# A transformer block on one core: the first chunk's normalization in an order written by hand, three MLP blocks ahead of the projections

## The chip, the cores and the metric

The kernel runs on one core of a Trainium2 chip. The core has a matrix engine (TensorE, PE in the profile; its weight loads are PEld), a vector engine (VectorE, DVE), a scalar engine (ScalarE, ACT), a general engine (GpSimd, POOL) and a queue engine (SyncE, SP) that issues most transfers. Each engine takes its instructions in the order in which they are written for it, and waits on semaphores for the others. SBUF is the on-chip memory, PSUM the accumulation memory that PE writes. The metric is the device time of one execution in microseconds (us).

## What is computed

x has 2048 rows of 1024 elements in bf16. It is normalized by rows, and the result goes into two branches: an attention of 32 heads in which each position sees eight earlier ones, two apart, and a gated MLP of width 3584.

```python
xn = _layernorm(x, axis=-1)                  # (x - mean) / sqrt(var + 1e-5)
s = _A_ref(xn, A_wqkv, A_wo)                 # qkv, 8 positions at distance 2, softmax, @ wo
g = _silu(_B_ref(xn, B_w1, B_w3, B_w2))      # silu((silu(xn@w1) * (xn@w3)) @ w2)
return x + s * g
```

## The kernel before

The rows are cut into four chunks of 512 (`CH`), each of four tiles of 128 rows. For a chunk the work is: `ln_transpose` (statistics and normalization of the four tiles, then eight 128x128 transposes on PE for each, copied by ACT into `xnT`, lines 122 to 140), `qkv` (24 accumulations `ps` of eight matmuls each, line 159, copied by ACT into qT, kT and vT, line 170), `attention` (on DVE: products `prod` and sums into `E`, lines 177 to 180; an exchange of partitions by GpSimd's transfers, line 184; the softmax, lines 188 to 201; transfers back, line 204; products with v summed into `oT`, lines 211 to 226), `wo_proj` (eight accumulations of eight matmuls, line 241, copied by ACT into `s_sb`, line 247), `mlp_up` (14 blocks; a block loads one tile of w1 and one of w3, fills four accumulations `gu` on line 264, and ACT's silu `sg` and DVE's product `ht` free them, lines 271 and 273), and `mlp_down_epilogue` (for both halves `dh` of the columns, four accumulations `acc_0_*` and `acc_1_*` of 28 matmuls each, line 324, and an `epilogue` for each).

An epilogue loads a piece `x_e` of x (line 281, GpSimd's queue), takes the silu of the accumulation on ACT into `gt` (line 289), multiplies by `s_sb` and adds `x_e` on DVE (lines 290 and 291), and stores `o_t` (line 292, GpSimd's queue). `x_e`, `gt` and `o_t` have two buffers each (the pool "ep").

The loop over chunks (lines 352 to 363) writes `ln_transpose` of the next chunk ahead of `mlp_down_epilogue`. The order on each engine isn't that of the text: a scheduler takes the instructions of the whole program and sets an order for each engine by its own estimate of when they are ready; `high_priority` moves some ahead. The order is then fixed. The accumulations of `mlp_up`, `qkv` and `mlp_down` share six banks of PSUM ("mm"), those of `wo_proj` and of the transposes two ("aux").

Chunk 0 differs. Its tiles are normalized one by one (`group=1`), and its first MLP block (`M1A = 1`) works in two halves of 256 columns (`nsplit=2`), so that it needs only two of the four tiles at first. Its projection weights come as six tiles `raw` (line 102; three buffers), which DVE and ACT permute in 24 copies of 128x1024 into three tiles `pm` (line 107); `qkv` of chunk 0 reads them from there, and three stores write them to DRAM as `wperm` (line 340) for the later chunks. Three further MLP blocks (`M1B = 4`) follow `qkv` before attention. Ahead of everything PE runs twelve matmuls on zeros (line 71).

Of the kernel before, what the change touches and what calls it, by code (L numbers as in the profile page):

```python
# [1 line left out]

# [5 lines left out]
FP32 = mybir.dt.float32  # L8
BF16 = mybir.dt.bfloat16
ACTF = mybir.ActivationFunctionType  # L10
ALU = mybir.AluOpType
# [4 lines left out]
def kernel(  # L16
# [11 lines left out]
    nc = tc.nc  # L28
    P = 128
    S, D, F = 2048, 1024, 3584  # L30
    Dh, W, DIL = 32, 8, 2
    KT = D // P
    CH = 512
    NCH = S // CH
    NST = CH // P
# [1 line left out]
    HALO = 16  # L37
    NWARM = 12
    M1B = 4
    M1A = 1  # L40
    NJ = 8
    NR = 4
    scale = float(Dh) ** -0.5

    x_flat = A_x.rearrange("b s d -> (b s) d")
    out_flat = out.rearrange("b s d -> (b s) d")
    w1_r = B_w1.rearrange("(kt p) f -> p kt f", p=P)
    w3_r = B_w3.rearrange("(kt p) f -> p kt f", p=P)
# [5 lines left out]
    psum_mm = ctx.enter_context(tc.tile_pool(name="psum_mm", bufs=6, space=bass.MemoryType.PSUM))  # L54
    psum_aux = ctx.enter_context(tc.tile_pool(name="psum_aux", bufs=2, space=bass.MemoryType.PSUM))
    ln = ctx.enter_context(tc.tile_pool(name="ln", bufs=2))
    small = ctx.enter_context(tc.tile_pool(name="small", bufs=4))
    xnT_pool = ctx.enter_context(tc.tile_pool(name="xnT", bufs=2))
    wstream = ctx.enter_context(tc.tile_pool(name="wstream", bufs=6))
# [3 lines left out]
    eps_t = const.tile([P, 1], FP32, name="eps_t")  # L63
    nc.vector.memset(eps_t[:], 1e-5)
    warm = const.tile([P, CH], BF16, name="warm")
    nc.vector.memset(warm[:], 0.0)
    scr = const.tile([P, 1], FP32, name="scr")
    nc.scalar.activation(out=scr[:], in_=eps_t[:], func=ACTF.Sqrt)
    wps = psum_aux.tile([P, CH], FP32, tag="aux", name="warm_ps")
    for _ in range(NWARM):  # L70
        nc.tensor.matmul(wps[:], lhsT=warm[:, 0:P], rhs=warm[:], start=True, stop=True)
    ident = const.tile([P, P], BF16, name="ident")
    nc.gpsimd.memset(ident[:], 0.0)
    nc.gpsimd.affine_select(
        out=ident[:], in_=ident[:], compare_op=ALU.not_equal, fill=1.0,
# [5 lines left out]
        out=maskb[0:32], in_=maskb[0:32], compare_op=ALU.is_ge, fill=-1.0e9,  # L81
# [9 lines left out]
    hp = ctx.enter_context(tc.tile_pool(name="hT", bufs=FT + 1))  # L91
    sgp = ctx.enter_context(tc.tile_pool(name="sg", bufs=3))
# [2 lines left out]

    wqkv_r = A_wqkv.rearrange("(kt kp) c -> kp kt c", kp=P)

    def permute_load(stage, t):
        pm = stage.tile([P, KT, NJ, P], BF16, tag="pm", bufs=3)
        for half in range(2):  # L100
            raw = stage.tile([P, 4, D], BF16, tag="raw", bufs=3)
            nc.sync.dma_start(out=raw[:], in_=wqkv_r[:, half * 4:(half + 1) * 4, t * D:(t + 1) * D])
            for k4 in range(4):
                kt = half * 4 + k4
                src = raw[:, k4, :].rearrange("k (h r j) -> k j r h", r=NR, j=NJ)
                dst = pm[:, kt, :, :].rearrange("k j (r h) -> k j r h", r=NR)
                PERM_ENG[(t * KT + kt) % len(PERM_ENG)](out=dst, in_=src)
        return pm

    PERM_ENG = [nc.vector.tensor_copy, nc.scalar.copy, nc.vector.tensor_copy]  # L110

    def ln_transpose(c, group=NST):
        xnT = xnT_pool.tile([P, KT, CH], BF16, tag="xnT")
        mv = small.tile([P, NST, nc.vector.BN_AGGR_DIM], FP32, tag="mv")
        rstd = small.tile([P, NST], FP32, tag="rstd")
        for st0 in range(0, NST, group):
            sts = range(st0, st0 + group)
            x_ts = {}
            for st in sts:
                g = c * NST + st  # L120
                x_t = ln.tile([P, D], BF16, tag="x_t", bufs=NST)
                nc.sync.dma_start(out=x_t[:], in_=x_flat[g * P:(g + 1) * P, :])
                stats = small.tile([P, 2, nc.vector.BN_STATS_DIM], FP32, tag="stats")
                for i in range(2):
                    nc.vector.bn_stats(out=stats[:, i, :], in_=x_t[:, i * 512:(i + 1) * 512])  # L125
                nc.vector.bn_aggr(out=mv[:, st, :], in_=stats[:])
                x_ts[st] = x_t
            sl = slice(st0, st0 + group)
            nc.scalar.activation(out=rstd[:, sl], in_=mv[:, sl, 1], func=ACTF.Sqrt, bias=eps_t[:], scale=1.0)
            nc.vector.reciprocal(out=rstd[:, sl], in_=rstd[:, sl])  # L130
            for st in sts:
                xn = ln.tile([P, D], BF16, tag="xn")
                nc.vector.tensor_scalar(
                    out=xn[:], in0=x_ts[st][:], scalar1=mv[:, st, 0:1], scalar2=rstd[:, st:st + 1],
                    op0=ALU.subtract, op1=ALU.mult,
                )
                tp = psum_aux.tile([P, KT, P], BF16, tag="aux")
                for kt in range(KT):
                    nc.tensor.transpose(tp[:, kt, :], xn[:, kt * P:(kt + 1) * P], ident[:])  # L139
                nc.scalar.copy(out=xnT[:, :, st * P:(st + 1) * P], in_=tp[:])  # L140
        return xnT

    def qkv(c, xnT, pms=None):
        if c > 0:
# [102 lines left out]
                    nc.scalar.copy(out=s_sb[:, st, dh * 512:(dh + 1) * 512], in_=ps[:])  # L247
        return s_sb

    def mlp_up(c, xnT, fb0, fb1, nsplit=1):  # L250
        hts = []
        cw = CH // nsplit
        for fb in range(fb0, fb1):
            w1t = wstream.tile([P, KT, 2 * P], BF16, tag="w")
            nc.sync.dma_start(out=w1t[:], in_=w1_r[:, :, fb * 256:(fb + 1) * 256])
            w3t = wstream.tile([P, KT, 2 * P], BF16, tag="w")
            nc.sync.dma_start(out=w3t[:], in_=w3_r[:, :, fb * 256:(fb + 1) * 256])
            pss = [psum_mm.tile([P, CH], FP32, tag="mm", name=f"gu{c}_{fb}_{k}") for k in range(4)]
            order = [(sp, k) for sp in range(nsplit) for k in range(4)] if nsplit > 1 else [(0, k) for k in range(4)]
            for sp, k in order:  # L260
                i, wt = k // 2, (w1t if k % 2 == 0 else w3t)
                cs = slice(sp * cw, (sp + 1) * cw)
                for kt in range(KT):
                    nc.tensor.matmul(  # L264
                        pss[k][:, cs], lhsT=wt[:, kt, i * P:(i + 1) * P], rhs=xnT[:, kt, cs],
                        start=(kt == 0), stop=(kt == KT - 1),
                    )
            for i in range(2):
                with tc.high_priority():
                    sg = sgp.tile([P, CH], BF16, tag="sg")  # L270
                    nc.scalar.activation(out=sg[:], in_=pss[2 * i][:], func=ACTF.Silu)
                    ht = hp.tile([P, CH], BF16, tag="ht")
                    nc.vector.tensor_mul(ht[:], sg[:], pss[2 * i + 1][:])  # L273
                hts.append(ht)
        return hts

    def epilogue(c, st, dh, acc, s_sb, nh=1):
# [51 lines left out]
                epilogue(c, st, dh, accs[st], s_sb)  # L329

    pools = {}
    xnT_cur = ln_transpose(0, group=1)
    hts0 = []
    with tc.tile_pool(name="stage", bufs=1) as stage:
        hts0 += mlp_up(0, xnT_cur, 0, M1A, nsplit=2)
        pms = [permute_load(stage, t) for t in range(3)]
        qkv(0, xnT_cur, pms)
        hts0 += mlp_up(0, xnT_cur, M1A, M1B)
        for t in range(3):
            nc.sync.dma_start(  # L340
                out=wperm[:, :, t * NJ:(t + 1) * NJ, :].rearrange("kt kp j p -> kp kt (j p)"),
                in_=pms[t][:].rearrange("kp kt j p -> kp kt (j p)"),
            )
# [8 lines left out]
    for c in range(NCH):  # L352
        if c > 0:
            qkv(c, xnT_cur)
        oT = attention(c)
        s_sb = wo_proj(c, oT)
        if c == 0:
            hts = hts0 + mlp_up(c, xnT_cur, M1B, FT // 2)
        else:
            hts = mlp_up(c, xnT_cur, 0, FT // 2)  # L360
        xnT_next = ln_transpose(c + 1) if c + 1 < NCH else None
        mlp_down_epilogue(c, hts, s_sb)
        xnT_cur = xnT_next

# [29 lines left out]
```

## Time and profile before

| | us |
|---|---|
| median of 3 runs (lowest, highest) | 841.57 (841.38, 841.77) |
| span of the profiled execution, first to last instruction | 841.2 |
| PE busy | 819.3 |
| DVE busy | 477.1 |
| ACT busy | 213.9 |
| POOL busy | 123.7 |
| mean granted clock of PE, as a share of full | 0.990 |

The profile shows one execution. Its span is 0.2 us below the lowest of the runs and 0.4 below their median; its own time with what lies around the span isn't given. A line of the timeline gives the start, the duration, the engine, the line of the kernel, the operation, what it writes and reads, the shape, the count, and in brackets how long the engine stood idle before it and what released it. A line of waits gives who waited for whom, the total, how often, and the longest. In a table of stretches each line has the stretch, its length, the busy time and number of instructions of PE, PEld, DVE, ACT and POOL, the granted clock, the share of the 16 DMA engines and GB/s.

Where the stages lie in the profiled execution:

| stage of chunk 0 | us from the start of the span |
|---|---|
| first matmul of MLP block 0 | 12.69 |
| qkv of chunk 0 on PE | 20.97 to 62.57 |
| MLP blocks 1 to 13 on PE | 62.41 to 159.47 |
| acc_0 and the first 52 matmuls of acc_1 | 159.47 to 194.90 |
| wo_proj | 194.90 to 208.71 |
| transposes of chunk 1 and the other 60 of acc_1 | 208.71 to 223.86 |
| qkv of chunk 1 begins | 223.86 |

### The profile page before, as it was taken

The page shows a single profiled execution, that of the slowest core. Times are in us where ns is not written, and L with a number is a line of the kernel's source. Part 1 is how long each engine was busy: PE and PEld are TensorE (multiplying, and loading weights), DVE is VectorE, ACT ScalarE, POOL GpSimd, SP SyncE. Part 2 cuts the span into 40 slices and gives each one's busy share as a digit, 9 for nine tenths or more (in the row PEclk, how much of TensorE's full clock was granted, in tenths as well). Part 3 has the DMA queues.
Part 4 walks back from the last instruction along what each step waited for, and adds up shares of the span by engine and source line. Part 5 has one row for each costly group of instructions (what it writes and reads, how often), then busy time and mean ns, then how long its engine had stood idle before and what let it go on. Part 6 is the DMA issues. An engine that isn't in the chain of part 4 may idle for free.

```text
span 841.2 us, 9707 instructions
## 1 busy us (share of the span) xinstructions
PE 819.3 (97%) x3884; PEld 377.0 (45%) x3884; DVE 477.1 (57%) x488; ACT 213.9 (25%) x325; POOL 123.7 (15%) x210
## 2 busy tenths in 40 slices
PE   7999889999999999999999999999999999999995
PEld 5444334444444444444444444444444444444442
DVE  7429946595239835494143955379302693629811
ACT  6742113103343113102233212210403311310120
POOL 1002133003100224002120040401102004120011
PEclk8999999999999999999999999999999999999998
DMA  9999397746595596754675577855476559593320
GB/s 302 314 358 230 102 226 173 190 150 176 130 289 149 153 201 183 177 164 119 193 239 150 148 170 185 202 154 167 114 213 200 151 150 200 159 205 112 109 81 25
DMA packets 208525, 149.54 MB, mean 178 GB/s; under 512 B 7776, under 2 KB 196192, under 8 KB 208480
## 3 DMA queue, kind: packets, MB, share of 16 engines
q1 hardware_dynamic: 201296, 132.14, 57.2%
q0 software_dynamic: 7184, 16.79, 8.0%
q8 instruction: 30, 0.49, 0.3%
q14 instruction: 15, 0.12, 0.1%
HBM read 130.02 MB, written 10.49 MB: 167 GB/s over the span
## 4 chain that ended last, share of the span: by engine, by line
PE 80%; DVE 15%; issue 3%; DMA 1%; ACT 0%; POOL 0%; POOLq 0%; DVEq 0%
PE ps L159 20%; PE ps L241 7%; DVE oT L226 2%; DVE B L225 2%; DVE C L211 2%; DVE B L211 2%; DVE ht L273 1%; DVE prod L177 1%; DMA x_t<-in_A_x_dram 1%; PE tp L139 1%; DVE oT L219 1%; PE acc_1_3_1668 L324 1%; PE acc_1_2_6323 L311 1%; PE acc_1_0_4763 L324 1%; PE acc_0_2_1505 L324 1%
## 5 line engine op out<-in xcount | busy, mean ns | idle before, releaser
L264 PEld LDWEIGHTS <-w3t 128*128 128x128 bf16 x912 | 89.8, 98 | 111.4 <-issue 7.8
L264 PEld LDWEIGHTS <-w1t 128*128 128x128 bf16 x912 | 89.6, 98 | 104.6 <-issue 0.2
L159 PE MATMUL ps<-xnT,wt 128*128 128x512 bf16 x576 | 124.8, 379 | 0.0
L324 PEld LDWEIGHTS <-ht 128*128 128x128 bf16 x784 | 76.4, 98 | 90.0 <-issue 0.2
L177 DVE TENSOR_TENSOR prod<-qT,kT 128x4096 bf16<-128x4096 bf16 x32 | 72.6, 2286 | 41.8 <-ACT kT L170 40.9
L159 PEld LDWEIGHTS <-wt 128*128 128x128 bf16 x576 | 56.3, 98 | 68.0
L290 DVE TENSOR_TENSOR gt<-gt,s_sb 128x512 f32<-128x512 f32 (+1 forms) x33 | 21.6, 673 | 77.0 <-ACT gt L289 64.3
L125 DVE BATCH_NORM_STATS2 stats<-x_t 128x6 f32<-128x512 bf16 x32 | 20.5, 671 | 58.4 <-DMA x_t<-in_A_x_dram 58.4
L204 POOL DMA_DIRECT2D E_persist<-pb x64 | 36.9, 584 | 100.1 <-DVE pb L201 93.3
L292 POOL DMA_DIRECT2D out_dram<-o_t x33 | 18.2, 551 | 205.9 <-DVE o_t L291 204.4
L159 PE MATMUL ps<-xnT,pm 128*128 128x512 bf16 x192 | 41.6, 379 | 0.0
L241 PEld LDWEIGHTS <-oT 128*128 128x128 bf16 x256 | 24.8, 98 | 32.9 <-DVE oT L226 3.4
L178 DVE TENSOR_TENSOR prod<-prod 128x2048 bf16<-128x2048 bf16 x32 | 38.4, 1219 | 0.0
L211 DVE TENSOR_TENSOR B<-E_persist,vT 128x4096 bf16<-128x4096 bf16 x16 | 36.5, 2284 | 0.0
L241 PE MATMUL ps<-wa,oT 128*128 128x512 bf16 x128 | 32.9, 379 | 1.9 <-DVE oT L226 1.9
L241 PE MATMUL ps<-wb,oT 128*128 128x512 bf16 x128 | 32.8, 379 | 0.0
L247 ACT CAST s_sb<-ps 128x512 bf16<-128x512 f32 x32 | 18.8, 586 | 48.5 <-PE ps L241 48.5
L159 PEld LDWEIGHTS <-pm 128*128 128x128 bf16 x192 | 18.8, 98 | 22.4
L291 DVE TENSOR_TENSOR o_t<-gt,x_e 128x512 bf16<-128x512 f32 (+1 forms) x33 | 21.6, 672 | 12.1 <-DMA x_e<-in_A_x_dram 11.8
L170 ACT CAST kT<-ps 128x512 bf16<-128x512 f32 x32 | 18.8, 586 | 36.5 <-PE ps L159 36.5
L226 DVE TENSOR_TENSOR oT<-oT,B 128x4096 bf16<-128x4096 bf16 x12 | 27.5, 2292 | 0.4
L170 ACT CAST vT<-ps 128x512 bf16<-128x512 f32 x32 | 18.7, 586 | 35.4 <-PE ps L159 35.4
(579 smaller groups left out, 1276.3 us busy)
## 6 DMA issues: line engine op xcount, KB each, us to landing
w1t<-in_B_w_dram SPq DMA_DIRECT2D x56, 512.0 KB, 4.3
w3t<-in_B_w_dram SPq DMA_DIRECT2D x56, 512.0 KB, 5.1
w2t<-in_B_w_dram SPq DMA_DIRECT2D x49, 512.0 KB, 3.5
wt<-wperm SPq DMA_DIRECT2D x36, 512.0 KB, 4.3
raw<-in_A_wqkv_dram SPq DMA_DIRECT2D x6, 1024.0 KB, 7.4
wperm<-pm SPq DMA_DIRECT2D x3, 2048.0 KB, 14.8
x_t<-in_A_x_dram SPq DMA_DIRECT2D x16, 256.0 KB, 5.6
wa<-in_A_wo_dram SPq DMA_DIRECT2D x32, 128.0 KB, 4.1
```

What stands on the lines that cost most here:

```text
L159: nc.tensor.matmul(ps[:], lhsT=lhsT, rhs=xnT[:, kt, :], start=(kt == 0), stop=(kt == KT - 1),)
L170: nc.scalar.copy(out=dst, in_=ps[:])
L177: nc.vector.tensor_mul(prod[:], qT[:], kT[:, :, o:o + CH])
L178: nc.vector.tensor_add(prod[:, 0:4, :], prod[:, 0:4, :], prod[:, 4:8, :])
L204: nc.gpsimd.dma_start(out=E[r * 32:(r + 1) * 32, :, sq * P:(sq + 1) * P], in_=pb[sq * 32:(sq + 1) * 32, :, :],)
L211: nc.vector.tensor_mul(dst, E[:, w, :].unsqueeze(1).to_broadcast([P, NJ, CH]), vT[:, :, o:o + CH])
L226: nc.vector.tensor_add(A, A, B[:])
L241: nc.tensor.matmul(ps[:], lhsT=oT[:, j, st * P:(st + 1) * P], rhs=(wa if j < 4 else wb)[:, j % 4, :], start=(j == 0), stop=(j == NJ - 1),)
L264: nc.tensor.matmul(pss[k][:, cs], lhsT=wt[:, kt, i * P:(i + 1) * P], rhs=xnT[:, kt, cs], start=(kt == 0), stop=(kt == KT - 1),)
L290: nc.vector.tensor_mul(gt[:, lc], gt[:, lc], s_sb[:, st, gc])
L291: nc.vector.tensor_add(o_t[:, lc], gt[:, lc], x_e[:, lc])
L324: nc.tensor.matmul(accs[st][:], lhsT=hts[f][:, st * P:(st + 1) * P], rhs=w2t[:, i, :], start=(f == 0), stop=(f == FT - 1),)
```

## The change

Three things are changed in chunk 0's beginning.

1. A new function `head` replaces `ln_transpose(0, group=1)` and block 0. Its instructions on PE, DVE and ACT stand in the program's order (`manual_schedule`). x tiles 0 and 2 are loaded over SP's queue, 1 and 3 over ACT's. Tile 1's sum and sum of squares are taken on ACT, by the accumulator of two activations. The transposes of tiles 2 and 3 stand between the first matmuls of block 0. After the transposes of tile 0, and again after those of tile 1, four matmuls on `xn` write into the bank of the first matmuls on zeros, which now is one of the six "mm" banks.
2. `M1A` is 3: MLP blocks 1 and 2 stand ahead of `qkv`, in the same written order, with the first eight permutes (and the loads for them) between them. The other sixteen permutes follow.
3. The loads of chunk 1's x are issued after the last `raw` load (`issue_after`), and all four tiles of a later chunk share one square root, as before.

```diff
-    M1A = 1
+    M1A = 3
...
+    def head():
...
+        def busy(src, n):
+            for _ in range(n):
+                nc.tensor.matmul(wps[:], lhsT=warm[:, 0:P], rhs=src[:, 0:CH], start=True, stop=True)
...
+        def part(k, h):
+            i, wt, cs = k // 2, (w1t if k % 2 == 0 else w3t), slice(h * 256, (h + 1) * 256)
+            for kt in range(KT):
+                nc.tensor.matmul(
+                    pss[k][:, cs], lhsT=wt[:, kt, i * P:(i + 1) * P], rhs=xnT[:, kt, cs],
+                    start=(kt == 0), stop=(kt == KT - 1),
                 )
...
+        for st in range(NST):
+            (nc.sync, nc.scalar)[st % 2].dma_start(out=x_ts[st][:], in_=x_flat[st * P:(st + 1) * P, :])
+        nc.sync.dma_start(out=w1t[:], in_=w1_r[:, :, 0:256])
+        nc.sync.dma_start(out=w3t[:], in_=w3_r[:, :, 0:256])
+        nc.scalar.activation(out=scr[:], in_=eps_t[:], func=ACTF.Sqrt)
+        half_stats(x_ts[0], stats[0], 0)
+        half_stats(x_ts[0], stats[0], 1)
+        aggr(0)
+        nc.scalar.activation(out=junk[:], in_=x_ts[1][:], func=ACTF.Identity, accum_out=tot[:])
+        nc.scalar.mul(out=nm[:], in_=tot[:], mul=-1.0 / (32.0 * D))
+        std(0)
+        half_stats(x_ts[2], stats[2], 0)
+        xn0 = norm(0)
+        tp0 = pe_transpose(xn0)
+        busy(xn0, 4)
+        nc.scalar.activation(
+            out=junk[:], in_=x_ts[1][:], func=ACTF.Square, bias=nm[:], scale=1.0 / 32.0, accum_out=mv[1][:, 1:2],
+        )
+        nc.scalar.mul(out=mv[1][:, 0:1], in_=tot[:], mul=1.0 / D)
+        std(1)
+        copy_in(tp0, 0)
+        half_stats(x_ts[2], stats[2], 1)
+        aggr(2)
+        std(2)
+        xn1 = norm(1)
+        tp1 = pe_transpose(xn1)
+        busy(xn1, 4)
+        copy_in(tp1, 1)
+        half_stats(x_ts[3], stats[3], 0)
+        xn2 = norm(2)
+        half_stats(x_ts[3], stats[3], 1)
+        aggr(3)
+        std(3)
+        xn3 = norm(3)
+        part(0, 0)
+        tp2 = pe_transpose(xn2)
+        copy_in(tp2, 2)
+        part(1, 0)
+        part(2, 0)
+        tp3 = pe_transpose(xn3)
+        copy_in(tp3, 3)
+        part(3, 0)
+        for k in range(4):
+            part(k, 1)
+        return xnT, pss
...
-    xnT_cur = ln_transpose(0, group=1)
-    hts0 = []
     with tc.tile_pool(name="stage", bufs=1) as stage:
-        hts0 += mlp_up(0, xnT_cur, 0, M1A, nsplit=2)
-        pms = [permute_load(stage, t) for t in range(3)]
+        with tc.manual_schedule(engines={mybir.EngineType.PE, mybir.EngineType.DVE, mybir.EngineType.Activation}):
+            xnT_cur, pss0 = head()
+            hts0 = [gate_up(pss0[2 * i], pss0[2 * i + 1]) for i in range(2)]
+            pms, perm = permuter(stage)
+            for fb in range(1, M1A):
+                for _ in range(4):
+                    next(perm)
+                hts0 += mlp_up(0, xnT_cur, fb, fb + 1)
+            for last_load in perm:
+                pass
         qkv(0, xnT_cur, pms)
...
-        xnT_next = ln_transpose(c + 1) if c + 1 < NCH else None
+        xnT_next = ln_transpose(c + 1, after=last_load if c == 0 else None) if c + 1 < NCH else None
```

`permuter` makes the same 24 permutes as `permute_load`, one at a call, on the same engines in turn; `gate_up` is the silu and product of a block, as before. With the program rebuilt, the scheduler's order changes in other places as well. On DVE the second half of chunk 1's and the first of chunk 2's preparation (a reciprocal, two normalizations, four statistics) stands ahead of chunk 0's attention and no longer behind its products. On PE all 112 matmuls of acc_1 of chunk 0 stand ahead of `wo_proj`, and the 32 transposes and qkv of chunk 1 follow it directly. On ACT the four silu of acc_1 stand between the `s_sb` copies of `wo_proj`.

## The prediction

> **What bounds the kernel now.** I read the page's first table, then what PE waited for, then three stretches of the timeline and the granted clock in them. PE is busy almost throughout:
>
> ```profile
> PE 819.3 (97%) x3884; PEld 377.0 (45%) x3884; DVE 477.1 (57%) x488; ACT 213.9 (25%) x325; POOL 123.7 (15%) x210
> ```
>
> So only the 22 us in which PE is idle (841.2 - 819.3), and matmuls at a reduced clock, can be won or lost. The head is the first place:
>
> ```profile
> 3.36 1.88 DVE L125 BATCH_NORM_STATS2 stats<-x_t 128x6 f32<-128x512 bf16 x3 [2.19 <-DMA x_t<-in_A_x_dram]
> ...
> 9.73 0.29 ACT L129 ACTIVATE rstd<-mv,eps_t 128x1 f32<-128x1 f32 x1 [0.51 <-DVE mv L126]
> ...
> 9.93 1.91 ACT L140 COPY xnT<-tp 128x1024 bf16<-128x1024 bf16 x2
> ...
> 12.69 1.91 PE L264 MATMUL gu_0_0_215<-xnT,w1t 128*128 128x256 bf16 x8
> ...
> 20.97 41.60 PE L159 MATMUL ps<-xnT,pm 128*128 128x512 bf16 x192
> ```
>
> (Columns: start, duration, instruction, idle time before it and its releaser.) ACT copies no transposed tile before the fourth square root is done at 10.02, although the first transposes ended at 7.68. The first useful matmul waits until 12.69. The second place is in the attention of chunk 0, in PE's list of waits:
>
> ```profile
> PE gu_5_3_1001 L264 <- DVE ht L273: 2.8, 1, 2.8
> PE gu_7_1_1095 L264 <- DVE ht L273: 2.8, 1, 2.8
> ```
>
> The second of these has a visible cause in DVE's timeline. DVE, which takes its instructions in order, stands twice before statistics of a later x tile, and the product `ht` that frees PE's bank is behind them:
>
> ```profile
> 105.78 1.28 DVE L125 BATCH_NORM_STATS2 stats<-x_t 128x6 f32<-128x512 bf16 x2 [2.32 <-DMA x_t<-in_A_x_dram]
> 109.46 0.69 DVE L125 BATCH_NORM_STATS2 stats<-x_t 128x6 f32<-128x512 bf16 x1 [2.40 <-DMA x_t<-in_A_x_dram]
> ...
> 110.74 0.67 DVE L273 TENSOR_TENSOR ht<-sg,gu_5_3_1001 128x512 bf16<-128x512 bf16 x1
> ```
>
> The granted clock is in the stretches (stretch and length, then busy time by engine, then clock):
>
> ```profile
> 5.07:8.48 3.41, 1.43 (x12) 0.64 (x10) 3.41 (x11) 0.59 (x2) 0.00 (x0) 1.00 1.13 317
> 8.48:11.90 3.42, 1.96 (x17) 1.74 (x18) 2.31 (x8) 2.40 (x4) 0.00 (x0) 0.50 1.06 369
> ...
> 93.82:97.24 3.42, 1.56 (x8) 0.59 (x6) 3.42 (x4) 0.00 (x0) 0.00 (x0) 1.00 0.04 12
> 107.47:110.89 3.42, 1.23 (x6) 0.48 (x5) 1.43 (x4) 0.00 (x0) 1.91 (x4) 1.00 1.13 249
> 110.89:114.30 3.41, 2.84 (x7) 0.99 (x7) 1.78 (x4) 0.60 (x1) 1.09 (x2) 0.50 1.16 207
> ```
>
> After a stretch of 3.4 us with 1.43 or 1.23 us of PE work the next stretch has half the clock. After 1.56 us of work (93.82 to 97.24) it stayed at 1.00 until 110.89. The head runs at half clock from 8.48 to 15.31, the attention of chunk 0 from 110.89 to 114.30.
>
> **The head, -2.5 us.** The x tiles come over two queues. Tile 0 landed 2.59 us after its issue, the four within 4.5; with tiles 0 and 1 side by side I take 3.9 for both instead of 3.33. From there, with durations of the rows: two statistics and aggregate to 5.45 (0.62 each in a run, 0.19); root on ACT 0.29, reciprocal 0.15, normalization 0.53, first transposes at 6.9 against 7.06. On ACT the sum of tile 1 takes 4.0 to 5.0 (no such row; the copy of 1024 elements takes 0.96, the exponential of 1024 took 1.06, so 0.9 to 1.3), the squares 5.8 to 6.8, small steps and root to 7.45, copy of tile 0 to 8.5, root of tile 2, copy of tile 1 to 10.1. DVE's tile 1 is normalized at 8.5, its transposes end at 9.1. Part (0,0) starts at 10.15. The eight fillers (4 x 0.216 twice at full clock) fill 7.5 to 8.4 and 9.1 to 10.0, inside waits, so they cost nothing unless the clock is at half: then 8 x 0.43, and part (0,0) starts near 12. With them the stretch 5.07 to 8.48 holds some 2.3 us of work, above 1.56, so I take the full clock. Eight parts of 0.87 (17.47 to 20.97 has four), the late transposes 2 x 0.55 and 0.2 for the last copy end at 18.4 instead of 20.9. Bounds: -3.2 (tile 0 lands as now) and -0.3 (half clock).
>
> The Trainium skill speaks against the two queues: "Trainium Kernel Development and Optimization", Key Constraints, says that transfers issued from different engines share the same 16 DMA engines, so several queues save issue time only. By it the second queue saves some 0.4 us of issue and delays tile 0. No run shows this yet.
>
> **Blocks 1 and 2 ahead of qkv, 0.** The 64 matmuls only change places (6.9 us per block), and qkv is now at 32.2 to 73.6. Its cover: `pm` for t=0 must be ready at 32.2; its last copies follow the silu of block 1 and end at about 28.3 on ACT (1.95 each) and DVE (1.03). On SP the raw loads are now interleaved with w1/w3; at the measured 0.3 to 0.39 MB per us the fifth raw lands near 35. ACT holds two of its permutes in front of the first qT copy, so the copies start near 39.5, and PE, with six banks, needs the first by 42.5: 3 us of cover. Chunk 1's x tiles, queued behind the three wperm stores (2 MB each), land near 60 and chunk 2's first two near 69, both before DVE has to start attention at 73.6. Taken as 0; without that cover 1 to 3 us.
>
> **Attention of chunk 0, -4.1 and +1.0.** DVE starts its products at the end of qkv as before, and its order to the first `ht` that PE waits for is the same one two blocks on, so the 2.8 us of the first stall return (at gu_7_3). At 0.46 of work its stretch kept the clock by a little; where the 2.8 us lie in the 3.41 us grid decides, so 0 or 1.4 (the row of 111.46: 3.11 until the next instead of 1.73); I take 1.0. The second stall goes: statistics and normalizations now stand ahead of the products. That is 2.76 plus 1.38 = 4.1. The `ht` that is late next, gu_6_3's, is needed 0.3 us after it is there.
>
> **The border to chunk 1, +5.7 and +2.5.** This is the cost that the diff does not show. In the changed program's order PE does all 112 matmuls of acc_1 before `wo`, then 64 `wo`, 32 transposes and directly qkv of chunk 1. Before, 52 of acc_1 came first and 60 lay between the transposes and qkv. And on ACT, in order, each `s_sb` copy is now behind a `gt` silu of acc_1, which waits until the epilogue two tiles earlier has let go its buffer; behind the copy PE waits for its bank. Now, the epilogue runs at the pace of the x_e loads:
>
> ```profile
> 201.42 0.54 POOL L281 DMA_DIRECT2D x_e<-in_A_x_dram  x1
> 202.35 0.69 DVE L291 TENSOR_TENSOR o_t<-gt,x_e 128x512 bf16<-128x512 f32 x1 [0.76 <-DMA x_e<-in_A_x_dram]
> ...
> 203.88 0.54 POOL L281 DMA_DIRECT2D x_e<-in_A_x_dram  x1
> 205.38 0.69 DVE L291 TENSOR_TENSOR o_t<-gt,x_e 128x512 bf16<-128x512 f32 x1 [1.74 <-DMA x_e<-in_A_x_dram]
> ...
> 206.91 0.54 POOL L281 DMA_DIRECT2D x_e<-in_A_x_dram  x1
> ...
> 208.71 0.61 PE L139 MATMUL tp<-ident,xn 128*128 128x128 bf16 x8
> 209.36 0.55 DVE L133 TENSOR_SCALAR xn<-x_t,mv,rstd 128x1024 bf16<-128x1024 bf16 x1 [3.29 <-PE tp L139]
> ```
>
> From issue to use 2.6 us (199.73 to 202.35) and 4.0 (201.42 to 205.38) alternate. Counting from the first `wo` matmul (194.90 = 0): `o_t` of tiles 2 and 3 end at 8.1 and 11.2 as now. Tile 4: after tile 3 and a 0.69 product, 12.55. Tile 5: x_e issued at 12.0, +4.0, ends 16.7. Tile 6: 18.1. In DVE's order `xn` of the third x tile comes only now: 18.65. On ACT silu 7 waits for tile 5: 17.3, copy 7 to 17.9, then the four xnT copies (0.95 each); the second transposes at 18.5, the fourth `xn` at 19.85, its transposes at 20.45, the last copy at 21.7. So qkv starts 21.7 after `wo`. Before it was 223.86 - 194.90 - 60 x 0.216 = 16.0 for the same work: +5.7. With all loads at 2.6 the same count gives 19.75 (+3.7); with the longest wait of this trace (227.67 to 232.94, 5.3) near 24 (+8). Until qkv starts, PE has some 7 us with 1.65 us of transposes: by the rows the clock falls, and qkv begins at half clock for one to two stretches of 3.41: 1.7 to 3.4, taken 2.5.
>
> Here the skill would say less: "TensorE: Matmul & The Clock Gate", Part 1, lets the clock fall after an idle window, and transposes in between are not idle. The row with 1.23 us of work contradicts it. By the page the sum would be 2.5 lower.
>
> Later chunks keep their order but for single instructions, so 0.
>
> **Sum.** -2.5 + 0 - 4.1 + 1.0 + 5.7 + 2.5 = +2.6. The profiled span of 841.2 becomes 843.8; the runs' median of 841.57 lies 0.4 above that span, so 844.2.
>
> **Rivals.** (a) *The epilogue does not hold up qkv*: ACT's silu and x_e come in time, the border costs at most +1 without a clock loss. Then -2.5 - 4.1 + 1 = -5.6: 836. For: x_e needs only 2.4 us at best. Against: ACT's and DVE's order are fixed, and chunk 0 needs six x_e loads in a chain of two buffers. It decides once eight epilogues fit into the 13.8 us of `wo`. (b) *Near balance*: x_e at 2.6 throughout, clock loss 1.7, none at the first stall: -2.5 - 4.1 + 3.7 + 1.7 = -1.2: 840.4. (c) *The queues of qkv 0 bind too*: raw or x tiles land 3 us later than worked out, ACT holds qT back or DVE starts attention late: +2.6 + 3 = 847. (d) *The head gains nothing*, since the clock stays at half: +2.6 + 2.2 = 846.4.
>
> **How the numbers follow.** Forecast (844.2, its own spread 842 to 846) 0.45; (a) 0.15; (b) 0.22; (c) 0.10; (d) 0.08. 0.2% is 1.7 us, about what a measurement tells from no change. Faster by that: (a) and a third of (b), 0.22; same: the rest of (b) and a small part of the forecast, 0.22; slower 0.56. The range leaves out (a) and part of (c): 838.5 to 848.5.
>
> **What would show it.** Right: part (0,0) near 10 at clock 1.00; no DVE wait for x_t near 105; PE idle 4 us or more between `wo` and qkv of chunk 1, released by `xn` or xnT, with clock 0.50 after it. Wrong: qkv of chunk 1 directly behind the transposes; PE waiting in qkv of chunk 0 or a half clock in the head.

## The result and the profile after

| | before | changed |
|---|---|---|
| median of the runs, us (lowest to highest, number) | 841.48 (840.40 to 841.77, 4) | 847.09 (846.34 to 847.49, 4) |
| ratio to before, 95% interval | | 1.0068 (1.0053 to 1.0084) |
| span of the profiled execution | 841.2 | 845.3 |
| PE busy | 819.3 | 817.4 |

The change costs 0.7%. That is slower by more than the 0.2% that the prediction takes for no change; the forecast of 844.2 was 2.9 us too low. The first table of the changed kernel's profile has on its PE line:

```profile
PE 817.4 (97%) x3817; PEld 376.7 (45%) x3892; DVE 476.0 (56%) x485; ACT 216.5 (26%) x331; POOL 123.5 (15%) x210
```

PE is busy 1.9 us less, so its idle time grew from 22 to some 28 us (75 of the changed kernel's 3892 matmuls have no record here, so the 28 are rather too many). The head did what the prediction worked out. Two rows of the changed kernel's timeline (start, duration, instruction, idle time before it and its releaser):

```profile
4.24 1.29 DVE L123 BATCH_NORM_STATS2 stats<-x 128x6 f32<-128x512 bf16 x2 [3.07 <-DMA x<-in_A_x_dram]
...
10.20 1.03 PE L192 MATMUL gu<-xnT,w_first 128*128 128x256 bf16 x8 [0.24 <-ACT xnT L198]
```

Tile 0 comes later than before (4.24 against 3.36), yet the first useful matmul runs at 10.20 and not at 12.69, and at the full rate: eight matmuls of 256 columns take 1.03 and not 1.91 for the first group. Block 0 ends at 18.46 (before 20.97). What is lost is in PE's list of waits (who waited for whom, total, times, longest; four of its lines):

```profile
PE tp L135 <- DVE xn L127: 3.0, 2, 1.6
PE gu L372 <- DVE ht L358: 2.8, 1, 2.8
...
PE tp L135 <- ACT s_sb L350: 2.2, 2, 1.6
...
PE ps L262 <- ACT xnT L159: 1.1, 1, 1.1
```

One of the two `ht` stalls of 2.8 is left. Of the first line 1.6 us are in the head; its other 1.3 and the two last lines whole stand in one place, between `wo` and qkv of chunk 1. The same place in the timeline of the changed kernel, where the first `wo` matmul is at 202.67:

```profile
213.87 0.69 DVE L394 TENSOR_TENSOR o_t<-gt,x_e 128x512 bf16<-128x512 f32 x1 [1.99 <-DMA x_e<-in_A_x_dram]
...
214.59 0.60 ACT L392 ACTIVATE gt<-acc 128x512 f32<-128x512 f32 x1 [2.20 <-DVE o_t L394]
...
215.09 0.58 ACT L350 CAST s_sb<-ps 128x512 bf16<-128x512 f32 x1
...
215.72 1.02 PE L344 MATMUL ps<-wa,oT 128*128 128x512 bf16 x4 [0.80 <-ACT s_sb L350]
...
222.39 2.09 PE L135 MATMUL tp<-ident,xn 128*128 128x128 bf16 x16 [1.34 <-DVE xn L127]
...
225.58 0.59 PE L262 MATMUL ps<-xnT,wt 128*128 128x512 bf16 x1 [1.10 <-ACT xnT L159]
```

Read it as a chain: `o_t` waits for its `x_e` load, the silu on ACT waits for `o_t` to give its buffer back, the `s_sb` copy stands behind that silu, and PE waits for the copy to free its bank. The additions of the tiles 2 to 6 all wait so for their loads, by 0.9 to 2.0 us. Then `xn` stands behind the same additions on DVE. Qkv starts 22.9 us after `wo`. In the kernel before, `wo` started at 194.90, and the timeline has for qkv of chunk 1:

```profile
223.69 41.60 PE L159 MATMUL ps<-xnT,wt 128*128 128x512 bf16 x192
```

That is 28.8 us after `wo`, 12.9 of them the 60 matmuls of acc_1 in between, so 15.8 for the same work. (The table ahead of the prediction has 223.86 for this start, and the prediction works out 16.0 with it; both are 0.17 too high.) Three stretches around the start of qkv in the changed kernel, laid so that the clock changes at their borders (stretch, length, busy time of PE, PEld, DVE, ACT and POOL, then the granted clock, the DMA share and GB/s):

```profile
219.17:222.58 3.41, 0.80 (x12) 0.62 (x12) 2.12 (x5) 2.91 (x4) 1.48 (x3) 1.00 0.45 157
222.58:225.99 3.41, 2.17 (x17) 1.47 (x16) 1.41 (x3) 2.02 (x2) 2.00 (x4) 0.50 0.34 115
225.99:229.40 3.41, 3.19 (x9) 1.21 (x9) 0.00 (x0) 0.21 (x1) 0.00 (x0) 0.50 0.12 38
```

After 0.80 us of PE work in 3.41 the clock is at half for two stretches, the second of them under qkv.

Stage by stage on PE, with a second profile of the kernel before, e7, which the experiments below explain:

| stage, us | before | before, e7 | changed | forecast |
|---|---|---|---|---|
| to the end of block 0 | 20.97 | 21.91 | 18.46 | 18.4 |
| blocks 1 to 13 and qkv of chunk 0 | 138.50 | 135.78 | 135.83 | 135.4 |
| acc_0, acc_1, `wo`, transposes | 64.22 | 64.23 | 71.29 | 69.9 |
| qkv of chunk 1 | 41.44 | 41.44 | 43.30 | 43.9 |
| the rest | 576.1 | 576.0 | 576.4 | 576.1 |
| span | 841.2 | 839.4 | 845.3 | 843.8 |

(The forecast column is the first one with the terms of the prediction added: -2.5, -3.1, +5.7, +2.5, 0.)

### The profile page after: what moved, and what is told of

It reads as the page before. It is cut to its first block, busy times and chain, and to the rows that moved or that the text cites. A ratio compares the mean times of both kernels' runs of the same rounds, so it can differ in the third digit from the quotient of the medians.

```text
span 845.3 us, 9649 instructions
## 1 busy us (share of the span) xinstructions
PE 817.4 (97%) x3817; PEld 376.7 (45%) x3892; DVE 476.0 (56%) x485; ACT 216.5 (26%) x331; POOL 123.5 (15%) x210
## 4 chain that ended last, share of the span: by engine, by line
PE 80%; DVE 14%; issue 3%; DMA 1%; ACT 1%; POOL 0%; POOLq 0%; DVEq 0%
PE gu L372 39%; PE ps L262 20%; PE acc L427 12%; PE ps L344 5%; DVE oT L329 2%; DVE B L328 2%; PE acc L414 2%; DVE B L314 2%; DVE C L314 2%; DVE prod L280 1%; DVE ht L358 1%; PE tp L135 1%; DMA x_e<-in_A_x_dram 1%; PE gu L192 1%; DVE prod L281 1%
## 5 line engine op out<-in xcount | busy, mean ns | idle before, releaser
L372 PE MATMUL gu<-xnT,w3t 128*128 128x512 bf16 x863 | 207.6, 381 | 3.6 <-DVE ht L358 2.8
L372 PE MATMUL gu<-xnT,w1t 128*128 128x512 bf16 x861 | 206.5, 380 | 1.0
L427 PE MATMUL acc<-w2t,ht 128*128 128x512 bf16 x767 | 170.3, 379 | 0.9
L358 DVE TENSOR_TENSOR ht<-sg,gu 128x512 bf16<-128x512 bf16 x112 | 76.8, 687 | 140.8 <-PE gu L372 126.2
L356 ACT ACTIVATE sg<-gu 128x512 bf16<-128x512 f32 x112 | 66.9, 597 | 282.5 <-PE gu L372 258.7
L372 PEld LDWEIGHTS <-w3t 128*128 128x128 bf16 x880 | 86.3, 98 | 107.4 <-issue 4.1
L372 PEld LDWEIGHTS <-w1t 128*128 128x128 bf16 x880 | 86.3, 98 | 104.3 <-issue 1.1
L392 ACT ACTIVATE gt<-acc 128x512 f32<-128x512 f32 (+1 forms) x33 | 18.4, 588 | 170.6 <-PE acc L427 140.6
L287 POOL DMA_DIRECT2D L<-E_persist x64 | 37.0, 585 | 74.8 <-DVE E_persist L283 65.7
L395 POOL DMA_DIRECT2D out_dram<-o_t x33 | 18.1, 549 | 194.8 <-DVE o_t L394 194.8
L123 DVE BATCH_NORM_STATS2 stats<-x_t 128x6 f32<-128x512 bf16 x24 | 15.3, 674 | 39.3 <-DMA x_t<-in_A_x_dram 39.3
L344 PE MATMUL ps<-wa,oT 128*128 128x512 bf16 x124 | 32.2, 379 | 3.2 <-DVE oT L329 2.4
```

Of the source, the lines that this page charges most:

```text
L287: nc.gpsimd.dma_start(out=L4[sq * 32:(sq + 1) * 32, r, :, :], in_=E[r * 32:(r + 1) * 32, :, sq * P:(sq + 1) * P],)
L344: nc.tensor.matmul(ps[:], lhsT=oT[:, j, st * P:(st + 1) * P], rhs=(wa if j < 4 else wb)[:, j % 4, :], start=(j == 0), stop=(j == NJ - 1),)
L356: nc.scalar.activation(out=sg[:], in_=g_ps[:], func=ACTF.Silu)
L358: nc.vector.tensor_mul(ht[:], sg[:], u_ps[:])
L372: nc.tensor.matmul(pss[k][:], lhsT=wt[:, kt, i * P:(i + 1) * P], rhs=xnT[:, kt, :], start=(kt == 0), stop=(kt == KT - 1),)
L427: nc.tensor.matmul(accs[st][:], lhsT=hts[f][:, st * P:(st + 1) * P], rhs=w2t[:, i, :], start=(f == 0), stop=(f == FT - 1),)
```

## The experiments

The theory after the result: the loss is all at the border between chunks 0 and 1, because two MLP blocks ahead of qkv are 13.8 us of matmuls that no longer lie between qkv and `wo`, so that the scheduler fills the wait for attention with all of acc_1 and has nothing left to put behind `wo`. The rivals: the epilogue is slow by itself, whatever the order; or the loss lies elsewhere. Ratios are to the kernel before, run on the same chip each time; its median was 840.4 to 840.9 there.

| run | median, us | ratio (95% interval) | profiled span |
|---|---|---|---|
| changed kernel | 847.09 | 1.0068 (1.0053 to 1.0084) | 845.3 |
| e1, 64 of acc_1 behind `wo` | 845.90 | 1.0061 (1.0048 to 1.0074) | 843.9 |
| e2, `M1A` = 1 | 840.81 | 0.9999 (0.9988 to 1.0009) | 839.2 |
| e3, x on one queue | 846.59 | 1.0065 (1.0050 to 1.0080) | 845.2 |
| e4, no fillers | 848.95 | 1.0094 (1.0076 to 1.0112) | 845.1 |
| e5, 32 of acc_1 behind `wo` | 836.12 | 0.9943 (0.9929 to 0.9956) | 834.3 |
| e6, `M1A` = 2 | 839.76 | 0.9982 (0.9970 to 0.9993) | 840.3 |
| e7, before, again | 841.19 (one run) | | 839.4 |
| e8, before with `M1A` = 3 | 849.75 | 1.0098 (1.0082 to 1.0114) | 848.6 |
| e9, no x_e loads | 839.90 | 0.9988 (0.9974 to 1.0002) | 838.1 |
| e10, e5 and the order of `ht` | 839.31 | 0.9978 (0.9967 to 0.9989) | 836.7 |
| e11, e10 and the order of softmax | 834.25 | 0.9921 (0.9907 to 0.9934) | 832.7 |

**e1: part of acc_1 back behind `wo`.** In `mlp_down_epilogue`, with `last_wo` the last matmul of `wo_proj`:

```diff
+                late = c == 0 and dh == 1 and fb >= 3
+                with tc.issue_after(last_wo[0].ins) if late else nullcontext():
                     (the matmuls of this fb)
```

> The changed kernel, but 64 of acc_1's 112 matmuls in chunk 0 may only be issued behind the last wo matmul; nothing else is touched. Theory (the cost lies in the border, because nothing is left for PE between wo and qkv of chunk 1): qkv of chunk 1 follows the transposes and 59 acc_1 matmuls without a wait; the 6.9 us of the border and the 1.9 us of half clock behind it go: span 845.3 - 8.8 = 836.5, time near 838.3, below the kernel before. Rival 1 (the epilogue chain is late by itself, at x_e's pace, and only hits another instruction: acc_1's banks come free late and qkv waits for them): 841 to 845. Rival 2 (the border is not where the time goes): 847, unchanged.

The border is as before (59 matmuls behind the transposes, no wait there), and nearly nothing is won. The timeline of e1 has the reason:

```profile
194.19 1.87 PE L346 MATMUL ps<-wa,oT 128*128 128x512 bf16 x4 [7.00 <-DVE oT L329]
```

Attention ends at 194.0 on DVE, in the changed kernel at 194.8: PE's order hardly moves it. With 48 acc_1 matmuls ahead of it PE reaches `wo` 7.0 us too early, and two stretches at half clock follow (192.6 to 199.4). The theory had the border right and its cure wrong: the wait had only been moved from one side of `wo` to the other.

**e2: one block ahead of qkv.**

```diff
-    M1A = 3
+    M1A = 1
```

> The changed kernel with M1A = 1: the new head, x tiles queued ahead of the wperm stores, but one MLP block ahead of qkv, as before. The scheduler then makes the old border by itself (52 acc_1 matmuls, wo, transposes, 55 more). Theory: the two moved blocks are needed for nothing but the head's permutes, and cost the border; the head keeps its -2.5, the second stall stays away (-4.1), the first returns with 0 to 1.7 of half clock: span 841.2 - 6.6 + 1 = 835.6 (834.6 to 836.3), time 836.0 to 837.4. Rival 1 (the blocks ahead of qkv, not the order of the x loads, removed the second stall): it is back, 4.1 more, span 839.7. Rival 2 (without blocks between them the head's permutes hold qkv of chunk 0): PE waits in qkv for pm, 2 us or more.

Rival 2 came, and the theory's number was missed by 3 to 5 us: the time is that of the kernel before. The old border is back without a wait, and so is what the blocks covered. A row of e2's timeline, the first projection of chunk 0:

```profile
20.46 2.31 PE L262 MATMUL ps<-xnT,pm 128*128 128x512 bf16 x7 [2.02 <-DVE pm L112]
```

Three waits for `pm`, 2.5 in all, eat the head's 2.5. The second stall doesn't come back (PE's list has one wait for an `ht`, 2.7), so rival 1 falls. The blocks are needed: with the faster head, qkv directly behind block 0 comes before its permuted weights. The eleven spans lie on two levels, five at 837.6 to 837.8 (mean clock 0.996 to 0.997) and six at 839.0 to 839.9 (0.992 to 0.994). In the profiled one, of the second group, a stretch at half clock lies behind the `ht` stall (98.6 to 102.8, 1.7 us lost), as in the changed kernel. So I read the two levels as executions with and without it; there is no trace of one without.

**e3: all x tiles of the head on SP.**

```diff
-            (nc.sync, nc.scalar)[st % 2].dma_start(out=x_ts[st][:], ...)
+            nc.sync.dma_start(out=x_ts[st][:], ...)
```

> The changed kernel with all four first x loads on SP. Theory (ACT's queue of loads costs twice: tile 0 shares its transfer, 4.24 against 3.36, and some 1.4 us are added outside the profiled span): tile 0's statistics start near 3.4, the head ends 0.4 to 0.9 earlier, and time minus span falls from 1.8 to 0.4: time 845.0. Rival 1 (the queue is innocent of what lies outside the span): 846.4, difference 1.8 kept. Rival 2 (tile 1 then lands later by as much as tile 0 gains, and ACT's sum of tile 1 is the critical one): the head ends as now or later, 847.

No difference that these runs can tell. In the trace tile 0's statistics start at 3.25 and not 4.24, but the first useful matmul at 10.31, 0.1 later. Tile 1 isn't what holds it: ACT's sum of tile 1 starts at 4.28 (4.41 with two queues), and tile 0's square root behind it is done at 5.85. But tile 2 lands later. Its first statistic stands ahead of tile 0's reciprocal in DVE's order, waits 0.96 us for the load and runs from 5.74 to 6.43, so tile 0 is normalized from 6.53 on (6.42 with two queues). So rival 2 has the outcome right, with another tile than the one it names. The theory's other half falls as well. Time minus span is 1.7 to 1.9 us in this and every run, the kernel before included: no queue adds to it.

**e4: no fillers** (`busy(xn0, 4)` and `busy(xn1, 4)` become 0).

> The changed kernel without the eight filler matmuls of the head. Theory (they keep the clock up: without them the stretch from 5 to 8.5 holds 1.3 us of PE work or less, where 1.43 was too little before): half clock for one stretch, the head ends 1.7 to 2.3 us later, time 848.8 to 849.4. Rival (they do nothing, since the clock needs something else): 847.1, clock 1.00 in the head without them. Rival 2 (they are in the way, the transposes of tile 1 wait behind them): 0.2 to 0.8 faster.

By the ratios 0.26% or 2.2 us slower than the changed kernel, as the theory has it; the two intervals overlap a little (1.0076 and 1.0084), so the size is uncertain. Two stretches of e4:

```profile
7.32:10.73 3.41, 1.48 (x18) 1.12 (x16) 2.94 (x9) 2.56 (x5) 0.00 (x0) 1.00 1.06 359
10.73:14.14 3.41, 3.41 (x22) 2.68 (x21) 0.71 (x2) 1.08 (x2) 0.00 (x0) 0.50 1.11 338
```

1.48 us of PE work in 3.41, and the next stretch is at half clock. In the changed kernel the first of these stretches has 3.17, and the next is at 1.00. qkv of chunk 0 starts at 33.8 and not 32.3. The profiled execution is among e4's two shortest: it has no half clock behind the `ht` stall.

**e5: 32 matmuls behind `wo`** (e1 with `fb >= 5`).

> The changed kernel with 32 of acc_1's matmuls kept behind wo in chunk 0 instead of 64 (80 ahead of it). Theory, as mended by the run with 64: DVE's attention ends near 194.2 whatever PE does, so wo can't start before that; 64 matmuls kept back left PE 7.0 us idle ahead of wo and 3.4 us more of half clock behind; 112 in front leave it idle behind wo. With 80 in front PE reaches 195.8 without a wait, and 27 to 32 matmuls (5.8 us) cover the copies of the transposes. Span 843.9 - 7.0 - 3.4, plus 1.7 if the half clock of the first stall returns: 833.5 to 835.2, time 835.3 to 837.0, 0.4 to 0.6% below the kernel before. Rival (the epilogue chain at x_e's pace is the bound, not the order): wo or qkv waits again by 3 us or more, 840 or above.

Right, in its number too: 836.12 was expected as 835.3 to 837.0. With 80 matmuls ahead of `wo`, PE gets there at 193.98 without a wait, and 27 matmuls cover the copies of the transposes. The first two waits of e5's list:

```profile
PE gu L374 <- DVE ht L360: 2.8, 1, 2.8
PE ps L346 <- DVE oT L329: 1.9, 3, 0.7
```

Two rows of e5's timeline, the starts of `wo` and of qkv of chunk 1:

```profile
193.98 1.03 PE L346 MATMUL ps<-wa,oT 128*128 128x512 bf16 x4
...
216.73 41.60 PE L262 MATMUL ps<-xnT,wt 128*128 128x512 bf16 x192
```

Nothing of the border is left. Qkv of chunk 1 starts 8.9 us earlier than in the changed kernel, and at full clock: from the first matmul of acc_0 (152.50) it is 64.23 us, as before, and not 71.29. The other 1.8 of the 8.9 lie ahead of acc_0, and 1.7 of them are a stretch at half clock behind the `ht` stall, which e5's profile doesn't have. This settles the border as the place of the loss: the same kernel, with nothing but the place of 32 matmuls changed, goes from 0.7% slower to 0.6% faster.

**e6: two blocks ahead of qkv** (`M1A` = 2).

> The changed kernel with M1A = 2. Theory: one block of 6.9 us is enough to cover the permutes that made PE wait 2.5 us in qkv of chunk 0 with M1A = 1, and takes away only 32 matmuls of cover ahead of wo, so that the scheduler itself leaves 28 matmuls behind the transposes: block 0 ends 18.4, qkv 25.3 to 66.9, 3.2 us less than with M1A = 1: span 836.0, time 837.8. Rival 1 (pm of a later t binds as well): a wait in qkv remains, time 839 to 840. Rival 2 (28 matmuls are too few to cover the border): a wait between wo and qkv of chunk 1 of 2 us or more and half clock behind it, 841 or more.

Neither the theory (837.8) nor its rivals: `pm` is there (0.2 us of wait, so rival 1 has the number and not the cause), the border is covered, and the time is 839.76 with runs from 836.9 to 842.1. The timeline of the profiled execution, the longest of them:

```profile
69.44 0.69 DVE L123 BATCH_NORM_STATS2 stats<-x_t 128x6 f32<-128x512 bf16 x1 [0.80 <-DMA x_t<-in_A_x_dram]
...
70.95 4.48 DVE L280 TENSOR_TENSOR prod<-qT,kT 128x4096 bf16<-128x4096 bf16 x2
...
106.46 3.57 PE L372 MATMUL gu<-xnT,w3t 128*128 128x512 bf16 x8 [5.96 <-DVE ht L358]
```

The last x tile ahead of attention, queued behind the three `wperm` stores, is waited for at 69.4; qkv ended at 67.5, so DVE starts its products 3.2 us late, and the `ht` stall grows from 2.8 to 6.0. With three blocks the same statistics are through at 72.4 and attention starts at 73.9. So in this execution the third block was missing as the cover of those x tiles; whether the shorter ones waited too, no trace shows. It is rival (c) of the prediction, which had the mechanism and missed that it binds at two blocks.

**e7: the kernel before, a second profile.** No edit.

> The kernel before, unchanged, for a second profile. Theory: the first profile's span of 841.2 was one of its longer executions (its other spans on this chip are 837.4 to 841.4, and time is 1.76 above the span in every run of every kernel), because a stretch of half clock or two more fell into it; a shorter execution shows the same waits (2.8, 2.8, 2.3, 1.9) and fewer stretches at half clock: span 838 to 839.7. Rival: the waits themselves differ (a load lands earlier and one of the two stalls is gone).

The rival holds. The span is 1.8 us shorter, and the second stall isn't there. Half clock is there as much as before, in the head and for one stretch in the attention; that stretch now lies behind the first stall (3.31 us from its first matmul to the next group, 1.72 in the first profile) and not behind the second. Its cause on DVE, in the timeline of e7:

```profile
108.98 0.69 DVE L125 BATCH_NORM_STATS2 stats<-x_t 128x6 f32<-128x512 bf16 x1 [1.13 <-DMA x_t<-in_A_x_dram]
...
110.25 0.67 DVE L273 TENSOR_TENSOR ht<-sg,gu 128x512 bf16<-128x512 bf16 x1
```

DVE waits 1.13 us for that x tile, where the first profile has 2.40; that is enough for `ht` to come in time. The tile was 1.3 us less late, and PE, whose head took 0.9 longer, needed the bank later. So the second stall hangs on when a load lands.

**e8: the old head with three blocks.** The kernel before with `M1A = 3`.

> The kernel before with M1A = 3 and nothing else: the old head, three blocks ahead of qkv, and with it the changed order at the border (all 112 acc_1 matmuls ahead of wo). Theory (the parts add): the head's 2.5 us are missing, everything behind is as in the changed kernel: 847.1 + 2.5 = 849.6. Rival 1 (the head's gain is lost further on, to the attention's end): the same as the changed kernel, 847. Rival 2 (x tiles or permutes come later than in the changed kernel, where they are interleaved by hand): 852 or more, with a wait in qkv of chunk 0 or the second stall back.

The parts add: 849.75, ratio 1.0098 against 1.0068, so the head is worth 0.30% or 2.5 us, as forecast, and the blocks alone cost about 1%. The two intervals touch (1.0082 and 1.0084), so the size is uncertain; in e8's trace qkv of chunk 0 starts 2.9 us later. `wo` to qkv of chunk 1 takes 23.0 here (205.77 to 228.73).

**e9: no x_e loads.**

```diff
-        x_e = pools["ep"].tile([P, 512], BF16, tag="x_e")
-        nc.gpsimd.dma_start(out=x_e[:], in_=x_flat[g0:g0 + P, cols0:cols0 + 512])
+        x_e = warm
```

> The changed kernel with every epilogue adding a constant tile in place of its x_e tile: the residual x is left out of the output, and the 32 x_e loads with it; the additions stay, and the order on PE, ACT and DVE is the changed kernel's. Theory (the border's 22.9 us are set by the x_e loads, one pair of buffers, 2.2 to 3.0 us a tile): the silus follow PE's matmuls, wo takes 13.9 us, two transposes and the last copies some 4 more, so qkv of chunk 1 starts about 18 after wo: span 845.3 - 4.9 = 840.4, or 838.5 if the 1.9 us of half clock go too; time 840.3 to 842.2. Rival (the order alone sets it, s_sb copies behind silus and xn behind seven epilogues, whatever the loads take): 22 or more after wo, time 846 to 847.

The span is 7.2 us shorter than the changed kernel's (6.7 by the ratios), though its order is the same. 3.2 are the border (19.7 after `wo` and not 22.9), 1.9 the half clock, which is gone, and 2.3 lie behind PE's last matmul (7.4 and not 9.7 to the span's end), which I hadn't expected and haven't followed up. So the rival falls, and the x_e loads are worth 3.2 of the 7.1 us by which the border grew (22.9 against 15.8). What is left is 1.7 longer than the theory's 18, and e9's timeline shows what comes next:

```profile
212.51 0.69 DVE L393 TENSOR_TENSOR o_t<-gt,warm 128x512 bf16<-128x512 f32 x1 [1.50 <-DMA out_dram<-o_t]
...
222.34 1.02 PE L262 MATMUL ps<-xnT,wt 128*128 128x512 bf16 x4 [1.23 <-ACT xnT L159]
```

The addition now waits for the store of `o_t` two tiles back, the next thing with two buffers. No run gives these tiles more buffers, so how the other 3.9 us divide between that store and the order isn't shown.

**e10: e5 and the first stall.** The products of w = 6 and 7 of chunk 0 are written behind blocks 4 to 6 and may only be issued behind an `ht`, and 88 matmuls are ahead of `wo`:

```diff
+            products(c, 0, 6)
+            hts0 += mlp_up(c, xnT_cur, M1B, 7)
+            products(c, 6, 7, after=last_ht[-2])
+            products(c, 7, 8, after=last_ht[-1])
```

> The run with 80 matmuls ahead of wo, and two more edits of order: in chunk 0 the products of w = 6 and 7 may only be issued behind ht of block 6, first and second half (these two ht stood behind five of attention's operations each, which made PE wait 2.8 us for a bank), and 88 instead of 80 acc_1 matmuls ahead of wo, since PE gets there earlier. Theory (what PE waits for in the first stall is DVE's order, not DVE's time): the stall of 2.8 us goes, and with it the half clock that falls behind it in some executions; attention ends near 193 as in the run before, PE reaches wo at 192.9: span 834.3 - 2.8 + 0 to 0.8 = 831.5 to 832.3, time 833.3 to 834.1. Rival (attention's end sets wo, and two ht more ahead of it push it on): the wait only moves ahead of wo, 835.5 to 836.5.

The rival's course, with a time worse than its 835.5 to 836.5: the stall of 2.8 is gone, and the time is 0.35% above e5 by the ratios. The wait came back ahead of `wo` (e10's timeline):

```profile
132.54 0.69 DVE L366 TENSOR_TENSOR ht<-sg,gu 128x512 bf16<-128x512 bf16 x1 [2.77 <-PE gu L380]
133.15 1.22 DVE L295 TENSOR_TENSOR z<-L 128x1024 f32<-128x1024 bf16 x1
...
196.49 1.87 PE L350 MATMUL ps<-wa,oT 128*128 128x512 bf16 x4 [3.58 <-DVE oT L333]
```

The order on DVE counts `ht` instructions, not time: the softmax's first addition `z` still stands behind the same number of them after the products, which now are later ones, and waits for an `ht` that PE gives only at 132.5. In e5 it started at 129.2. Attention ends at 196.3 and not 193.4.

**e11: the order of the softmax.** Added to e10, with `behind` a list of instructions that the silu and `ht` of a half block may only be issued behind:

```diff
+            behind.update({(11, 0): [z3], (11, 1): [mxi], (12, 0): [sub], (12, 1): [pbi, ex]})
```

> The last run with the order of chunk 0's softmax mended: there z stood one ht further back (behind that of block 11's first half, which PE gives only at 132.5), so attention ended at 196.3 instead of 193.3 and PE waited 3.6 us ahead of wo. Now the ht of block 11 may only be issued behind the third z addition and the maximum, those of block 12 behind the subtraction and pb, and the silu of 12's second half behind the exponential. Theory (wo is set by attention's end, and that by what stands ahead of z and the exponential in DVE's and ACT's order): attention ends at 193.3 to 194 again, PE waits 0.4 to 1.1 ahead of wo and keeps its clock: span 836.7 - 2.5 to 3.2 - 1.7 = 831.8 to 832.5, time 833.6 to 834.3. Rival (z is held up by the landing of L4, which comes 1 to 2 us later with the earlier ht, and pb's way back as well): attention ends at 195 or later, time 836 to 837, no better than with 80 matmuls alone.

834.25, inside 833.6 to 834.3. e11's timeline:

```profile
129.81 1.22 DVE L295 TENSOR_TENSOR z<-L 128x1024 f32<-128x1024 bf16 x1
...
194.22 1.02 PE L352 MATMUL ps<-wa,oT 128*128 128x512 bf16 x4 [1.20 <-DVE oT L335]
```

No `ht` stall, 1.2 us ahead of `wo`, and no half clock until the end of the kernel. This version has the changed head and three blocks, and is 0.8% faster than the kernel before.

## Why the prediction was right, and where its numbers were off

**The head, -2.5: right.** 18.46 at the end of block 0 (18.4 forecast), and e8 gives 2.5 by the ratio. Against e7 it is 3.4. The fillers were needed for it (e4); the stretch from 5.07 to 8.48 held 1.78 us of PE work and not the 2.3 worked out, which was still enough. On the two queues the Trainium skill's "Trainium Kernel Development and Optimization", Key Constraints, which says that they share the 16 DMA engines and save issue time only, agrees with the trace: 4.24 against 3.25 for tile 0, and no gain at the head's end.

**Blocks 1 and 2 ahead of qkv, 0: right at this place.** qkv of chunk 0 runs from 32.28 to 73.72 (32.2 to 73.6) without a wait. The cover I named, 3 us for the permutes, was real (2.5 us of waits without it, e2); that for the x tiles was thinner than I wrote (e6).

**Attention of chunk 0, -4.1 + 1.0 = -3.1: the sum nearly, by luck, the parts not.** Measured against the profile I worked from it is -2.7. The second stall's 2.76 went. The 1.38 of half clock that I added to it didn't: in the changed kernel a stretch at half clock behind the remaining stall costs 1.7 us (1.6 in e7). Against e7 this term is 0, since that execution has no second stall. The step that failed is "The second stall goes": it took a stall of one execution for the kernel's. What DVE stood before for 2.40 us was the landing of a load, and nothing said how steady that was. (`issue_after` isn't needed for this: e8 doesn't have it, and PE's list there too has one wait for an `ht`, 3.0.)

**The border, +5.7: the mechanism right, the size +7.1.** Matmuls ahead of `wo`, silus between the `s_sb` copies, the x_e loads' pace (e9, for 3.2 us of it), `xn` behind the additions: all seen. The step that was mis-sized is the chain of additions: from tile 2 to tile 6 they start 3.28, 2.51, 2.21 and 2.59 apart, where I had alternated long and short loads, by two values, and let the tiles 4 and 6 wait for nothing; so tile 6 ended 19.2 after `wo` and not 18.1; the rest of the chain is as counted within 0.1. What I did not see is why the order is so. Attention's end hardly moves with PE's order of acc_1 (194.0 in e1, 193.4 in e5, 194.8 here), the blocks moved away are 64 matmuls of cover ahead of it, and the scheduler filled up from behind (e1, e5).

**Half clock at qkv, +2.5: +1.9**, inside its bounds of 1.7 and 3.4.

**Later chunks, 0: +0.3**; the waits for `oT` are 2.4 and not 1.9.

**From span to time, 0.4: this failed.** The terms above sum to +4.1 and not +2.6 in the span, 1.5 of the 2.9 us missed. The rest is the step that added 0.4 to the span. Time minus span is 1.7 to 1.9 us in every run here, so the profiled execution of before took some 843.0 us, 1.4 above its median. It was a long one, and the second stall is what it had more. As far as two profiles tell, most of the 2.7 us of attention was not there to be won at the median.

Of the rivals, (a) and (b) fell with the border; (d) did not come; (c) is real at two blocks (e6), not at three. Its 847 is the time measured, by accident: qkv of chunk 0 has no wait, and DVE stands ready 1.5 us before attention can start.

## What to carry to other kernels

When work moves ahead of a stage, ask what it covered where it was: here 13.8 us of matmuls had covered attention, the price came 130 us later, where the filling was taken from another wait, and it went away when the filler was divided by the time at which the slow engine is ready (80 and 32 matmuls). An edit of order on one engine shifts what is counted behind it, so look for the instruction that now stands behind a later producer (e10). Before a stall that ends with a load's landing is counted as a gain, see a second execution: it may not be there.

## What the runs showed of the hardware

The granted clock falls after a stretch of 3.41 us with part of the work, not only after an idle one. In stretches laid so that it changes at their borders, it fell after 0.80 us of PE work (changed kernel), 1.23 and 1.43 (before) and 1.48 (e4), and stayed at 1.00 after 1.56 (before, 93.82 to 97.24) and 1.78 (e4, 3.91 to 7.32). From half it came back after a stretch with 2.84 (before, 110.89 to 114.30) or 3.41 (e4), and stayed down for a second after 1.96 (before, 8.48 to 11.90) or 2.17 (changed kernel). The Trainium skill's "TensorE: Matmul & The Clock Gate", Part 1, says for the start of a kernel that the window is free-running, so that the count of slow matmuls differs from run to run. In the middle of the kernel the two profiles of the kernel before show the like behind their first stall (1.72 and 3.31 us to the next group of matmuls), and the two levels of e2 would fit it. So the same stall of 2.8 us costs 2.8 in one execution and 4.5 in another: blocks 3 to 13 of chunk 0 take 78.9 us in e5's profile and 80.6 in the changed kernel's.

The sum over a row by ACT's accumulator takes an instruction of its own to read it: in the changed kernel 1.06 us for the sum of 1024 elements and 0.19 for reading the accumulator.

Without the 32 x_e loads the span ended 7.4 us after PE's last matmul and not 9.7, though no addition there waits for an x_e in the changed kernel's timeline; this isn't explained.
